# Convolving the first two 512-row blocks in eight 64x32 tiles of the matrix engine

## The chip, the cores and the metric

The kernel runs on one core of one Trainium2 chip. A core has a matrix engine (PE, with its weight loads shown as PEld), a vector engine (DVE), a scalar engine (ACT), GpSimd (POOL), and SyncE (SP), which only issues transfers. Results of PE land in PSUM, other data in SBUF. ACT, SP and POOL issue transfers too, each in the order of its own instruction stream, and a transfer that waits for something holds up what stands behind it on that engine.

The metric is the device time of one execution, in microseconds; the median of several runs is given. All times on a line of the profile are counted from the start of the profiled span.

## The reference

`x` is 8 x 4096 x 192 in float32. Each of 8 heads (24 channels each) has a filter of 7 taps, made by a softmax over its row of `weight`; a causal convolution along the sequence is followed by a gated feed-forward layer:

```python
w = np.exp(weight - np.max(weight, axis=-1, keepdims=True))
w = w / (np.sum(w, axis=-1, keepdims=True) + 1e-09)
x_pad = np.concatenate([np.zeros((B, pad, D)), x], axis=1)       # pad = 6
x_unf = x_pad[:, idx, :].reshape(B, S, K, H, group)              # 7 shifted rows
x = np.einsum('hk,bskhg->bshg', w, x_unf).reshape(B * S, D)      # 32768 x 192
gate = np.maximum(x @ w_gate, 0.0)                               # 192 -> 1536
val = x @ w_val
out = gate * val @ w_out                                         # 1536 -> 192
```

## The kernel before

The sequence is worked in 16 units of two windows of 512 rows, and every window holds two streams (batch b and batch b+4) on the two 64-row halves of the partitions. For each window the gate and value products are computed for 12 blocks f of the hidden dimension (`gate_val`, L602): per f, twelve matmuls for the gate and twelve for the value fill two PSUM tiles (in the first unit six and six, L621, each 64x128), ACT takes the ReLU of the gate (L632), DVE multiplies it with the value (L633). There are four PSUM tiles in turn, so block f+2 writes where block f was read. Then `project_turn` (L643) multiplies with `w_out`.

From the third window on the convolution is done by DVE, ACT and POOL on transposed x. The first two windows (blocks 0 and 1 below) cannot wait for that: they are convolved on PE (`conv_steps`, L370), with x as it lies in memory (rows on the partitions, channels along the free axis) as the stationary operand and a band matrix as the moving one. A band of head h has the seven taps along its diagonal. Window columns go in five steps of 106 (`STEP`), each from 112 rows of x (106 and 6 of the halo). A matmul takes one stream, one step and 32 channels, and writes 32 partitions of PSUM: a 128x32 tile, four of them side by side (`tile_position=(0, p0)`). Each group of 32 channels lies in two heads and is computed once with each head's band, the second over the first. That makes 5 steps x 3 chunks of 64 channels x 8 = 120 matmuls a block. One PSUM bank holds a chunk's 512 columns; an eviction (`evict`, L395) copies it to float16: for block 0 ACT, DVE, ACT, for block 1 ACT three times.

The order around it is written out by hand (manual schedule). At the start SP and ACT issue the five float32 pieces of x of block 0 (`load_raw`, L106; tiles prod1 to prod5), and ACT casts them to float16 (`cast`, L118). SP and ACT draw their transfers' semaphores from a ring of eight, DMAHW0 to DMAHW7; a ninth transfer waits until the first user of its semaphore has landed. Meanwhile the taps' exponential is taken on ACT (L278), DVE makes the products `prod`, `blk`, `blocks` (L287 to L299) from it, PE assembles the bands of eight heads by 24 matmuls (L335) in three PSUM parts, and DVE copies them out (L343). Block 0 is then convolved (L713), evicted, and feeds `gate_val`. Block 1 is convolved inside `gate_val` before block f = 10 (`CONV1`, L605). Its x is loaded by POOL in two transfers (one a stream, L97) that stand between the copies which double the weights onto the upper partitions (`pool_halves`, L233). `conv(2)` (L414) uses the same bands as stationary operand for the window after that.

Of the kernel before, what the change touches and what calls it, by code (L numbers as in the profile page):

```python
# [9 lines left out]
F16 = mybir.dt.float16  # L10
# [5 lines left out]
def kernel(  # L16
# [29 lines left out]
    GSUB = 5  # L46
    WARM = [(4, 4, 4, 1), (4, 3)]
    STEPS0 = [1, 0, 2, 3, 4]
    CONV1 = 10


# [29 lines left out]
    def staged(i, j):  # L81
        return stages[i][:, XH * j : XH * (j + 1)]

    def load_x(g, streams=range(2)):


        bp, toks = GROUPS[g]
        xt = staged(g // 3, g % 3).rearrange("p (j s d) -> p j s d", s=2, d=D)
        step = toks[1] - toks[0]
        rows = -(-(step + PAD) // 16) * 16  # L90
        for st in streams:
            src = bass.AP(
                tensor=x.tensor,
                offset=x.offset + ((bp + NB * st) * S + toks[0] - PAD) * D,
                ap=[[D, rows], [step * D, len(toks)], [1, D]],
            )
            nc.gpsimd.dma_start(out=xt[0:rows, 0 : len(toks), st, :], in_=src)  # L97
        return xt

    xts = {0: staged(0, 0).rearrange("p (j s d) -> p j s d", s=2, d=D)}  # L100
    ROWS = [SUB + PAD, 112, 112, 112, 96]
    raw = [
        apool.tile([128, 2 * LPOOL], FP, name=f"prod{jj + 1}")[:, 0 : 2 * D] for jj in range(GSUB)
    ]

    def load_raw(queue, jj):  # L106
        lo = STEP * jj - PAD
        p0 = max(0, -lo)
        queue.dma_start(
            out=raw[jj][p0 : ROWS[jj], :].rearrange("p (s d) -> p s d", s=2),  # L110
            in_=bass.AP(
                tensor=x.tensor,
                offset=x.offset + (lo + p0) * D,
                ap=[[D, ROWS[jj] - p0], [NB * S * D, 2], [1, D]],
            ),
        )

    def cast(copy, jj):  # L118
        copy(
            out=xts[0][0 : ROWS[jj], jj, :, :].rearrange("p s d -> p (s d)"),  # L120
            in_=raw[jj][0 : ROWS[jj], :],
        )

    HR = 128 // H
# [2 lines left out]
    nc.scalar.activation(out=early[:], in_=nc.const_aps.tensor(0.0, [128, 1], FP), func=ACTF.Exp)  # L127
    w8 = const.tile([H, KW], FP)
    nc.sync.dma_start(out=w8[:], in_=weight)
# [5 lines left out]
    nc.vector.memset(zeros[:], 0.0)  # L135
# [25 lines left out]
    with nc.allow_low_precision("one of the terms is not zero"):  # L161
        nc.vector.tensor_reduce(
            out=Z[:, 112 : 112 + HR],
            in_=eye[:].rearrange("p (g i) -> p i g", i=HR),
            axis=mybir.AxisListType.X,
            op=ALU.add,
        )
# [39 lines left out]
    raised = [raised[0][:, 0, :], raised[1][:, 0, :], held[:, 1, :]]  # L207
    for part, heads in zip(raised, BANDS):
        nc.tensor.matmul(
            out=part[:, 0 : SUB * len(heads)],  # L210
            lhsT=zeros[:],
            rhs=none(len(heads), SUB),
            start=True,
            stop=False,
            skip_group_check=True,
        )
# [106 lines left out]
    lane_load(0, range(1, 2))  # L323
    for jj in STEPS0[3:]:
        cast(nc.scalar.copy, jj)

    bands = [const.tile([128, len(heads), SUB], F16, name=f"band{heads[0]}") for heads in BANDS]
    for part, heads, to, copy in zip(
        raised, BANDS, bands, [nc.vector.tensor_copy] * 3
    ):  # L330
        n = len(heads)
        for j in range(128 // HR):
            s0 = HR * j - PAD
            lo, hi = max(0, -s0), min(BW, SUB - s0)
            nc.tensor.matmul(  # L335
                out=part[:, 0 : SUB * n].rearrange("p (h t) -> p h t", t=SUB)[:, :, s0 + lo : s0 + hi],
                lhsT=Z[:, 112 - HR * j : 240 - HR * j],
                rhs=blocks[:, heads[0] : heads[0] + n, lo:hi],
                start=False,
                stop=(j == 128 // HR - 1),  # L340
                skip_group_check=True,
            )
        copy(out=to[:].rearrange("p h t -> p (h t)"), in_=part[:, 0 : SUB * n])  # L343

    tap = const.tile([128, NCH, KW], FP)

# [18 lines left out]
            both_halves(nc.sync.dma_start, 10, Wv)  # L365

    def band(h):
        return bands[h // 3][0 : SUB + PAD, h % 3, :]

    dense, xcs = {}, {}  # L370

# [5 lines left out]
    def conv_steps(g, ps, c, steps):  # L377


        for jj in steps:  # L380
            col = STEP * jj
            n = min(STEP, WIN - col)
            rows = n + PAD
            for second in range(2):
                for st in range(2):
                    for k2 in range(2):
                        k = 2 * c + k2
                        h0, h1 = 32 * k // G, (32 * k + 31) // G
                        h, m = (h0, G * h1 - 32 * k) if second else (h1, 32)
                        p0 = 64 * st + 32 * k2  # L390
                        nc.tensor.matmul(  # L391
                            out=ps[p0 : p0 + m, 0, col : col + n],
                            lhsT=xts[g][0:rows, jj, st, 32 * k : 32 * k + m],
                            rhs=band(h)[0:rows, 0:n],
                            start=True,  # L395
                            stop=True,
                            tile_position=(0, p0),
                            skip_group_check=True,
                        )

    def evict(copy, g, ps, c):
        copy(out=dense[0][:, g, c, :], in_=ps[:, 0, :])  # L402

    def conv(g):

# [304 lines left out]
    for c, steps in (  # L710
        (0, STEPS0[:3]), (1, STEPS0[:3]), (0, STEPS0[3:4]), (1, STEPS0[3:4]), (0, STEPS0[4:]), (1, STEPS0[4:]), (2, STEPS0)
    ):
        conv_steps(0, first[c], c, steps)  # L713
    both_halves(nc.vector.tensor_copy, 0, Wg)
    both_halves(nc.vector.tensor_copy, 0, Wv)
    for c, copy in enumerate((nc.scalar.copy, nc.vector.tensor_copy, nc.scalar.copy)):
        evict(copy, 0, first[c], c)
# [85 lines left out]
```

## Time and profile before

| what | value |
|---|---|
| median of three runs | 762.4 us (761.5 to 762.61) |
| the profiled execution's own time | 762.03 us |
| its span | 760.3 us |
| PE busy | 756.3 us (99%) |
| DVE busy | 675.5 us (89%) |
| ACT busy | 610.0 us (80%) |
| POOL busy | 461.5 us (61%) |
| first matmul of the feed-forward part | at 7.98 us |
| block 1 convolved | from 21.11 us, 1.60 us |

The span is what lies between the first and the last instruction of the trace; the execution's own time is 1.7 us more. In the chain of waits each piece was released by the piece before it. In a timeline, a row has the start, the duration, the engine, line and operation, the number of instructions merged into it, and in brackets how long the engine stood idle before and what released it. The rows named SPq, ACTq and POOLq are issues of transfers, not their landings.

### The profile page before, as it was taken

How to read it: one execution, taken by the hardware profiler on the slowest of the kernel's cores; microseconds unless marked ns; L12 is line 12 of the kernel's file. 1: busy time of each engine (PE TensorE's matmuls, PEld its weight loads, DVE VectorE, ACT ScalarE, POOL GpSimd, SP SyncE). 2: the span in 40 equal slices, each digit the busy share in tenths (PEclk: the TensorE clock that was granted, in tenths of full speed). 3: DMA queues.
4: the chain of work that ended last, by engine and by line, in shares of the span. 5: the costliest groups of instructions: out<-in, count | busy, mean ns of one | idle time of the engine just before them, and what ended most of it. 6: DMA issues, size and time to landing. Idle time of an engine off the chain costs nothing.

```text
span 760.3 us, 30529 instructions
## 1 busy us (share of the span) xinstructions
PE 756.3 (99%) x13723; PEld 457.7 (60%) x13723; DVE 675.5 (89%) x647; ACT 610.0 (80%) x680; POOL 461.5 (61%) x311
## 2 busy tenths in 40 slices
PE   9999999999999999999999999999999999999998
PEld 5555555566666666666666666666666666666658
DVE  7889989998998989989999899998999989897891
ACT  7897887878878788887877878788797887877671
POOL 8729649195591946829377392874919659193600
PEclk9999999999999999999999999999999999999999
DMA  9953532345324443334434324352233532240302
GB/s 142 139 66 91 80 85 46 43 96 75 85 44 52 98 66 85 54 62 83 60 85 71 66 67 55 85 85 73 52 49 93 77 86 44 23 100 9 85 2 85
DMA packets 153714, 54.07 MB, mean 71 GB/s; under 512 B 148912, under 2 KB 153584, under 8 KB 153584
## 3 DMA queue, kind: packets, MB, share of 16 engines
q1 hardware_dynamic: 117152, 37.61, 21.8%
q0 software_dynamic: 35808, 14.07, 16.3%
q8 instruction: 107, 1.75, 1.0%
q10 hardware_dynamic: 624, 0.44, 0.2%
q14 instruction: 23, 0.19, 0.1%
HBM read 28.98 MB, written 25.17 MB: 71 GB/s over the span
## 4 chain that ended last, share of the span: by engine, by line
PE 99%; DVE 0%; ACT 0%; issue 0%
PE ps L621 65%; PE ps L643 31%; PE ps L686 2%; PE ps L391 0%; PE ps L193 0%; PE ps L335 0%; PE ps L414 0%; ACT xc L402 0%; PE ps L203 0%; DVE prod L287 0%; ACT out_s L697 0%; DVE blk L294 0%; DVE blocks L299 0%; ACT e L278 0%; DVE mx L275 0%
## 5 line engine op out<-in xcount | busy, mean ns | idle before, releaser
L633 DVE TENSOR_TENSOR hT<-gr,ps 128x1024 f16<-128x1024 f16 (+1 forms) x385 | 468.9, 1218 | 35.8 <-ACT gr L632 8.7
L632 ACT ACTIVATE gr<-ps 128x1024 f16<-128x1024 f32 (+1 forms) x385 | 392.8, 1021 | 114.7 <-PE ps L621 114.6
L550 POOL TENSOR_TENSOR prod<-prod,prod 128x896 f32<-128x896 f32 x145 | 302.8, 2088 | 251.3 <-DVE prod L584 242.2
L621 PE MATMUL ps<-xc,Wg 64*64 64x512 f16 (+1 forms) x4464 | 318.6, 376 | 0.2 <-ACT xc L402 0.2
L621 PE MATMUL ps<-xc,Wv 64*64 64x512 f16 (+1 forms) x4464 | 318.6, 376 | 0.0
L643 PE MATMUL ps<-hT,Wo 64*64 64x512 f16 x4320 | 235.8, 376 | 0.0
L621 PEld LDWEIGHTS <-Wv 64*64 64x64 f16 (+1 forms) x4464 | 150.0, 106 | 98.7 <-DVE hT L633 0.3
L621 PEld LDWEIGHTS <-Wg 64*64 64x64 f16 (+1 forms) x4464 | 146.6, 107 | 102.0
L643 PEld LDWEIGHTS <-Wo 64*64 64x64 f16 x4320 | 138.5, 107 | 94.4
L538 ACT ACTIVATE prod<-x_r,tap 128x1024 f32<-128x1024 f16 (+2 forms) x195 | 182.7, 1017 | 0.0
L574 DVE SCALAR_TENSOR_TENSOR acc<-x_r,tap,acc 128x1024 f32<-128x1024 f16 (+3 forms) x150 | 118.0, 853 | 0.0
L661 DVE STREAM_TRANSPOSE out_s<-ps 128x1024 f32<-128x1024 f32 x45 | 56.1, 1248 | 28.4 <-PE ps L643 24.4
L550 POOL TENSOR_TENSOR xc<-prod,prod 128x896 f16<-128x896 f32 x29 | 60.7, 2092 | 2.3
L479 POOL COPY x_p<-x_e 128x1536 f16<-128x1536 f16 (+1 forms) x32 | 42.2, 1349 | 0.0
L251 POOL DMA_DIRECT2D x_e<-in_x_dram x30 | 26.6, 890 | 0.0
L574 DVE SCALAR_TENSOR_TENSOR xc<-x_r,tap,acc 128x1024 f16<-128x1024 f16 (+3 forms) x30 | 25.2, 839 | 0.0
L563 ACT ACTIVATE acc<-x_r,tap 128x1024 f32<-128x1024 f16 (+3 forms) x30 | 22.5, 801 | 0.0
L656 ACT COPY turned_by<-ps 128x2 f32<-128x2 f32 x45 | 7.0, 154 | 16.8 <-PE ps L643 14.8
L686 PEld LDWEIGHTS <-hT 128*128 128x128 f16 x192 | 15.8, 98 | 0.4 <-issue 0.4
L686 PE MATMUL ps<-Wo,hT 128*128 128x192 f16 x192 | 16.0, 246 | 0.0
L697 ACT COPY out_s<-ps 128x768 f32<-128x768 f32 (+2 forms) x5 | 3.2, 638 | 12.7 <-PE ps L686 12.7
L697 DVE COPY out_s<-ps 128x192 f32<-128x192 f32 x1 | 0.4, 357 | 13.3 <-PE ps L686 13.3
(61 smaller groups left out, 74.6 us busy)
## 6 DMA issues: line engine op xcount, KB each, us to landing
out_dram<-out_s SPq DMA_DIRECT2D x125, 192.0 KB
x_e<-in_x_dram POOLq DMA_DIRECT2D x28, 384.0 KB, 5.8
x_r<-x_p SPq DMA_TRANSPOSE x116
prod<-in_moe_w_out_dram POOLq DMA_DIRECT2D x1, 576.0 KB, 9.1
out_dram<-out_s SPq DMA_DIRECT2D x5, 96.0 KB
out_s<-in_x_dram POOLq DMA_DIRECT2D x2, 210.0 KB, 6.2
out_s<-in_x_dram POOLq DMA_DIRECT2D x2, 192.0 KB, 6.6
x_e<-in_x_dram POOLq DMA_DIRECT2D x2, 192.0 KB, 3.8
```

The lines of the kernel that those rows point to most:

```text
L251: nc.gpsimd.dma_start(out=xe[:, 0:n, st, :, :].rearrange("p j c r -> p j (c r)"), in_=bass.AP(tensor=x.tensor, offset=x.offset + row * D, ...
L479: nc.gpsimd.tensor_copy(out=xp[:, js, :, st, :], in_=xe[:, js, st, :, :])
L538: nc.scalar.activation(out=both(prods[b, k], b, at, n), in_=shifted(b, c, k, t, n), func=ACTF.Copy, scale=tap[:, c, k : k + 1],)
L550: nc.gpsimd.tensor_tensor(out=acc if k < KW - 1 else xcs[b][:, w, :, :].rearrange("p c t -> p (c t)")[:, LDVE : NCH * WIN], in0=acc, in1=p ...
L563: nc.scalar.activation(out=both(accs[b], b, at, n), in_=shifted(b, c, 0, t, n), func=ACTF.Copy, scale=tap[:, c, 0:1],)
L574: nc.vector.scalar_tensor_tensor(out=result(b, at, n) if k == KW - 1 else both(acc, b, at, n), in0=shifted(b, c, k, t, n), scalar=tap[:, c ...
L621: nc.tensor.matmul(out=pss[i][q : q + M, st, :], lhsT=W[64 * st : 64 * st + 64, c, 128 * f + q : 128 * f + q + M], rhs=xcb[64 * st : 64 * ...
L632: nc.scalar.activation(out=gr[:, sts], in_=pss[0][:, sts], func=ACTF.Relu)
L633: nc.vector.tensor_tensor(out=h[:, f, sts], in0=gr[:, sts], in1=pss[1][:, sts], op=ALU.mult)
L643: nc.tensor.matmul(out=ps[64 * st : 64 * st + 64, b, :], lhsT=Wo[64 * r : 64 * r + 64, f, p, :], rhs=hs[b][64 * r : 64 * r + 64, f, st, :] ...
L661: nc.vector.transpose(out=o[:].rearrange("p t (b d) -> p b t d", b=2)[:, :, :, 32 * p : 32 * p + 32], in_=ps[:].rearrange("p b (t c) -> p ...
L686: nc.tensor.matmul(out=ps[:, i // 2, D * (i % 2) : D * (i % 2) + D], lhsT=h[:, f, st, 128 * q : 128 * (q + 1)], rhs=Wo[:, f, :, :].rearran ...
```

## The change

Blocks 0 and 1 are convolved with 64-row pieces. A window of 512 columns is cut into two halves of 256 (`HALF`); each half is cut into five pieces of 58 columns (`PIECE`, the last one 24), and each piece needs 64 rows of x (58 and 6). Pieces of the first half lie on partitions 0 to 63 and those of the second on 64 to 127, so a matmul takes one of eight 64x32 tiles, `tile_position=(64 * r, p0)`. The halves go to different PSUM banks. There are 240 matmuls a block in place of 120, of 58 (or 24) columns in place of 106 (or 88).

The band is built at 58 columns a head (`near`), for both partition halves at once (a copy of the identity block in `Z`, columns 176 on, does this): 12 matmuls in place of 24. The wide band that `conv(2)` needs (`large`) is cleared by DVE at the start and filled by two transfers on SP from `near`.

x of block 0 comes in ten transfers in place of five. The first has 58 rows (64 less the halo of 6, which is set to zero). The last two steps are cast for stream 0 by ACT and for stream 1 by DVE. x of block 1 comes in four POOL transfers in place of two. Block 1's second chunk is evicted by DVE in place of ACT.

```diff
-    ROWS = [SUB + PAD, 112, 112, 112, 96]
+    LAST = 64 + HALF - PIECE * (GSUB - 1) + PAD
+    ROWS = [64 + PIECE + PAD] * (GSUB - 1) + [LAST]
...
-    def load_raw(queue, jj):
-        lo = STEP * jj - PAD
+    def load_raw(queue, jj, r):
+        lo = HALF * r + PIECE * jj - PAD
         p0 = max(0, -lo)
+        n = min(64, -(-(ROWS[jj] - 64) // 32) * 32) if r == 0 else ROWS[jj] - 64
         queue.dma_start(
-            out=raw[jj][p0 : ROWS[jj], :].rearrange("p (s d) -> p s d", s=2),
+            out=raw[jj][64 * r + p0 : 64 * r + n, :].rearrange("p (s d) -> p s d", s=2),
...
-    for queue, steps in ((nc.scalar, (1, 2)), (nc.sync, (0, 3, 4))):
-        for jj in steps:
-            load_raw(queue, jj)
+    for queue, pieces in (
+        (nc.scalar, ((1, 0), (1, 1), (2, 0), (2, 1))),
+        (nc.sync, ((0, 0), (0, 1), (3, 0), (3, 1), (4, 0), (4, 1))),
+    ):
+        for jj, r in pieces:
+            load_raw(queue, jj, r)
...
+    large = const.tile([128, H, SUB], F16, name="large")
+    nc.vector.memset(large[:], 0.0)
+    nc.vector.memset(raw[GSUB - 1][32:64, :], 0.0)
...
+    nc.vector.tensor_copy(out=Z[:, 176 : 176 + HR], in_=Z[:, 112 : 112 + HR])
...
-    xts[1] = load_x(1, range(1))
+    xts[1] = load_x(1, halves=((0, 0), (1, 0)))
     for s in (3, 4, 5):
         pool_halves(s)
-    load_x(1, range(1, 2))
+    load_x(1, halves=((0, 1),))
     for s in (6, 7):
         pool_halves(s)
+    load_x(1, halves=((1, 1),))
     lane_load(0, range(1))
...
     for jj in STEPS0[3:]:
-        cast(nc.scalar.copy, jj)
+        cast(nc.scalar.copy, jj, slice(0, 1))
...
-        copy(out=to[:].rearrange("p h t -> p (h t)"), in_=part[:, 0 : SUB * n])
+        nc.vector.tensor_copy(
+            out=near[:, heads[0] : heads[0] + n, :].rearrange("p h t -> p (h t)"), in_=part[:, 0 : PIECE * n]
+        )
+    for jj in STEPS0[3:]:
+        cast(nc.vector.tensor_copy, jj, slice(1, 2))
+
+    for t in range(0, SUB, PIECE):
+        n = min(PIECE, SUB - t)
+        nc.sync.dma_start(out=large[t : t + n + PAD, :, t : t + n], in_=near[0 : n + PAD, :, 0:n])
...
-                        nc.tensor.matmul(
-                            out=ps[p0 : p0 + m, 0, col : col + n],
-                            lhsT=xts[g][0:rows, jj, st, 32 * k : 32 * k + m],
-                            rhs=band(h)[0:rows, 0:n],
...
-                            tile_position=(0, p0),
...
+                        for r in range(2):
+                            nc.tensor.matmul(
+                                out=ps[p0 : p0 + m, r, col : col + n],
+                                lhsT=xts[g][64 * r : 64 * r + rows, jj, st, 32 * k : 32 * k + m],
+                                rhs=near[64 * r : 64 * r + rows, h, 0:n],
...
+                                tile_position=(64 * r, p0),
...
-                    conv_steps(1, ps, c, range(GSUB))
-                    evict(nc.scalar.copy, 1, ps, c)
+                    conv_halves(1, ps, c, range(GSUB))
+                    evict_halves((nc.scalar.copy, nc.vector.tensor_copy)[c % 2], 1, ps, c)
```

How the change moves instructions is seen at three places. A row has the line, the operation, output and input tiles, the output's shape, and the semaphores that the instruction waits for (DVE_49 and its like are the engines' own counters). The first place is the start of SP's stream. In the names `prod_86` to `prod_90` are the five pieces' tiles, steps 0 to 4. Before:

```order
L129 DMA w_93<-in_weight_dram 8x7
L109 DMA prod_86<-in_x_dram 112x2x192
L109 DMA prod_89<-in_x_dram 112x2x192
L109 DMA prod_90<-in_x_dram 96x2x192
L354 DMA tap<-wn 24x1x7 [waits Pool_49]
```

After the change:

```order
L144 DMA w_93<-in_weight_dram 8x7
L124 DMA prod_86<-in_x_dram 58x2x192
L124 DMA prod_86<-in_x_dram 64x2x192
L124 DMA prod_89<-in_x_dram 64x2x192 x2
L124 DMA prod_90<-in_x_dram 32x2x192 [waits DMAHW0_49]
L124 DMA prod_90<-in_x_dram 30x2x192 [waits DMAHW2_49]
L372 DMA large<-near 64x8x58 [waits DMAHW3_49,DVE_49]
L372 DMA large<-near 60x8x54 [waits DMAHW4_49]
L383 DMA tap<-wn 24x1x7 [waits DMAHW5_49,Pool_49]
```

The weight takes DMAHW0, the 58-row piece DMAHW1 and the 64-row piece behind it DMAHW2, so the last two pieces of x wait for landings, and two transfers stand ahead of the taps. The second place is the start of ACT's stream. Before:

```order
L109 DMA prod_87<-in_x_dram 112x2x192
L109 DMA prod_88<-in_x_dram 112x2x192
L278 ACTIVATE e<-ps,mx 128x7 [waits DVE_49]
L281 ACTIVATE total,sm<-e 128x8 [waits Activation_49]
L119 CAST out_s<-prod_87 112x384 [waits DMAHW3_49]
```

After the change:

```order
L124 DMA prod_87<-in_x_dram 64x2x192 x2
L124 DMA prod_88<-in_x_dram 64x2x192
L124 DMA prod_88<-in_x_dram 64x2x192 [waits DMAHW1_49]
L300 ACTIVATE e<-ps,mx 128x7 [waits DVE_49]
L303 ACTIVATE total,sm<-e 128x8 [waits Activation_49]
L134 CAST out_s<-prod_87 128x384 [waits DMAHW5_49,DMAHW3_49]
```

The fourth transfer that ACT issues waits for DMAHW1, the semaphore of SP's 58-row piece; the exponential stands behind it. The third place is DVE's stream from block 0's eviction to beyond block 1. Before:

```order
L402 CAST xc<-ps 128x512 [waits PE_49]
L231 COPY Wg<-Wg 64x3x128 [waits DMASW2_49]
L231 COPY Wv<-Wv 64x3x128 [waits DMASW3_49]
L633 TENSOR_TENSOR hT<-gr,ps 128x512 [waits PE_49,Activation_49]
L633 TENSOR_TENSOR hT<-gr,ps 128x512 [waits Activation_49]
L633 TENSOR_TENSOR hT<-gr,ps 128x1024 [waits PE_49,Activation_49] x9
L611 MEMSET ps 128x1 [waits DVE_49]
```

After the change:

```order
L430 CAST xc<-ps 128x512 [waits PE_49]
L253 COPY Wg<-Wg 64x3x128 [waits DMASW2_49]
L253 COPY Wv<-Wv 64x3x128 [waits DMASW3_49]
L663 TENSOR_TENSOR hT<-gr,ps 128x512 [waits PE_49,Activation_49]
L663 TENSOR_TENSOR hT<-gr,ps 128x512 [waits Activation_49]
L663 TENSOR_TENSOR hT<-gr,ps 128x1024 [waits PE_49,Activation_49] x9
L430 CAST xc<-ps 128x512 [waits PE_49]
L641 MEMSET ps 128x1 [waits DVE_49]
```

An eviction of block 1 now stands on DVE between the product of block f = 9 and the one-element write that passes a PSUM tile on.

More of the change, by code (lines that the diff above doesn't have):

```diff
@@ L48 @@
     STEPS0 = [1, 0, 2, 3, 4]
+    HALF = WIN // 2
+    PIECE = 58
     CONV1 = 10
@@ L209 @@
         nc.tensor.matmul(
-            out=part[:, 0 : SUB * len(heads)],
+            out=part[:, 0 : PIECE * len(heads)],
             lhsT=zeros[:],
-            rhs=none(len(heads), SUB),
+            rhs=none(len(heads), PIECE),
             start=True,
@@ L324 @@
     for jj in STEPS0[3:]:
-        cast(nc.scalar.copy, jj)
[L327 to L330, printed above, removed]
+        cast(nc.scalar.copy, jj, slice(0, 1))
+    near = const.tile([128, H, PIECE], F16, name="near")
+    for part, heads in zip(raised, BANDS):
         n = len(heads)
-        for j in range(128 // HR):
+        for j in range(64 // HR):
             s0 = HR * j - PAD
-            lo, hi = max(0, -s0), min(BW, SUB - s0)
+            lo, hi = max(0, -s0), min(BW, PIECE - s0)
             nc.tensor.matmul(
-                out=part[:, 0 : SUB * n].rearrange("p (h t) -> p h t", t=SUB)[:, :, s0 + lo : s0 + hi],
+                out=part[:, 0 : PIECE * n].rearrange("p (h t) -> p h t", t=PIECE)[:, :, s0 + lo : s0 + hi],
                 lhsT=Z[:, 112 - HR * j : 240 - HR * j],
@@ L367, in band @@
     def band(h):
-        return bands[h // 3][0 : SUB + PAD, h % 3, :]
+        return large[0 : SUB + PAD, h, :]
     dense, xcs = {}, {}
@@ L375, with conv_halves @@
     PLACE |= {6: (1, 0, 0), 7: (1, 0, 1), 2: (1, 1, 0), 5: (1, 1, 1)}
[L377 to L382, printed above, removed]
+    def conv_halves(g, ps, c, pieces):
+        for jj in pieces:
+            col = PIECE * jj
+            n = min(PIECE, HALF - col)
             rows = n + PAD
@@ L712 @@
     ):
-        conv_steps(0, first[c], c, steps)
+        conv_halves(0, first[c], c, steps)
     both_halves(nc.vector.tensor_copy, 0, Wg)
@@ L716 @@
     for c, copy in enumerate((nc.scalar.copy, nc.vector.tensor_copy, nc.scalar.copy)):
-        evict(copy, 0, first[c], c)
+        evict_halves(copy, 0, first[c], c)
     both_halves(nc.vector.tensor_copy, 1, Wg)
```

37 lines of the change are left out of this document (25 added, 12 removed).

## The prediction

> **What bounds the kernel now.** First the page's totals and its chain of waits:
>
> ```profile
> span 760.3 us, 30529 instructions
> PE 99%; DVE 0%; ACT 0%; issue 0%
> ```
>
> PE sets the end nearly alone, so only what stands ahead of its unbroken run can change, or what PE itself does. The chain in order of time, over the first 24 us, shows both:
>
> ```profile
> 3.15 0.28 ACT e L278
> 3.45 0.33 DVE prod L287
> ...
> 4.57 1.22 PE ps L335 x24
> 5.78 1.54 PE ps L391 x70
> ...
> 7.35 0.59 ACT xc L402
> ...
> 7.98 13.20 PE ps L621 x120
> 21.18 1.53 PE ps L391 x120
> ```
>
> The exponential (3.15), the products, the bands, block 0 and its first eviction follow on each other; at 7.98 the feed-forward part starts, and block 1 takes 1.53 us out of it. So the sum has four terms: when the exponential starts, how long it is from there to the first L621, at what rate PE then runs, and what block 1 costs. It is made against the profiled execution's own 762.03 us, 0.37 below the median.
>
> **The exponential.** It is on ACT, behind ACT's transfers. After the change the fourth of these waits until SP's 58-row piece has landed, and behind it stand the exponential, the row sum and all casts; DVE's products, the bands and block 0 wait for these. The timeline:
>
> ```profile
> 0.81 0.41 SPq L129 DMA_DIRECT2D w<-in_weight_dram  x1
> 0.88 0.90 ACTq L109 DMA_DIRECT2D prod<-in_x_dram  x2
> 1.28 1.34 SPq L109 DMA_DIRECT2D prod<-in_x_dram  x3
> 2.32 0.50 PEld L203 LDWEIGHTS ps<-w,rows 8*128 8x128 f32 x2 [0.52 <-POOL prod L159]
> 3.66 0.50 ACT L119 CAST out_s<-prod 112x384 f16<-112x384 f32 x1
> 4.75 1.75 ACT L119 CAST out_s<-prod 118x384 f16<-118x384 f32 x4 [0.60 <-DMA prod<-in_x_dram]
> ...
> q10 hardware_dynamic: 624, 0.44, 0.2%
> ```
>
> A tiny transfer (the weight) is issued at 0.81 and used at 2.32: at most 1.51 us from issue to landing. ACT's queue q10 carried 624 packets in 0.2% of 16 engines' 760.3 us, 39 ns each. The 58-row piece is issued at 1.28 and has 58 x 2 = 116 packets. Spread evenly over 16 engines it lands at 1.28 + 1.51 + 0.3 = 3.1; cut into equal shares it has only two, 58 packets each, and lands at 1.28 + 1.51 + 2.3 = 5.1; if the 16 packets that ACT's pieces put on the same engines go in between, at 5.7. The kernel's pieces so far (112 and 96 rows) all have 16 equal shares, so no row decides. I take 5.1: the weight's 8 rows and the pieces fit equal shares, and 58 is the first count here that has hardly any. Then ACT issues its transfer (0.45, half of the row's 0.90), and the exponential starts at 5.55 in place of 3.15: **+2.4** (+0.4 to +3.0).
>
> [...]
>
> Ahead of that, DVE has two more clearings, the wide band (448 words a partition) and 384 more, and a 16-column copy:
>
> ```profile
> 0.89 0.11 DVE L135 MEMSET zeros<- 128x64 uint32 x1 [0.89 <-PEq L787]
> 1.97 0.37 DVE L162 TENSOR_REDUCE Z<-eye 128x16 f16<-128x128 f32 x1 [0.96 <-POOL Z L158]
> 5.15 1.22 DVE L343 CAST band<-ps 128x336 f16<-128x336 f32 x3 [0.25 <-PE ps L335]
> ```
>
> 64 words take 0.11, so 832 take at most 1.4 us, of which 0.96 is idle now. The rest delays POOL's weight loads by half a microsecond at most; the later exponential hides it. Without that cover it is part of the first rival.
>
> **From the exponential to the first L621.** PE's own rows at the start:
>
> ```profile
> 2.33 0.59 PE L203 MATMUL ps<-w,rows 8*128 8x7 f32 x2
> 2.85 0.93 PE L193 MATMUL ps<-const-bfloat16-1.0 128*128 128x512 bf16 x2
> 3.57 0.95 PE L209 MATMUL ps<-zeros 128*128 128x336 f16 x3
> 5.71 2.12 PE L391 MATMUL ps<-band,out_s 112*32 112x106 f16 x120
> ```
>
> It is 2.56 us to the first conv matmul (5.71) now. Half of the first band's eight matmuls go (4 x 1.22/24 = 0.2), and its copy has 174 columns in place of 336 (162 x 1.22/896 = 0.2): 2.2, so block 0 starts at 7.75. From there it is 2.27 us to 7.98 now: 1.62 to the end of the first chunk's matmuls, 0.59 eviction, the rest handing over. The rate of one matmul, by windows:
>
> ```profile
> 5.70:6.95 1.25, 1.25 (x63) 1.24 (x64) 1.14 (x4) 0.80 (x2) 1.25 (x3) 1.00 1.13 116
> 6.95:7.75 0.80, 0.80 (x76) 0.73 (x64) 0.31 (x1) 0.40 (x1) 0.80 (x2) 1.00 0.97 87
> 21.10:22.64 1.54, 1.54 (x122) 1.45 (x120) 1.47 (x2) 1.32 (x3) 1.54 (x3) 1.00 1.18 106
> ```
>
> The same matmuls pass at 19.8 ns each up to 6.95 and at 10.5 after it: PE runs at half speed first, though the page's clock column says 1.00. An eight-tile matmul has 58/106 of the columns and twice the tiles: 0.27 of that, 5.4 ns slow and 2.9 ns fast, if nothing but the array counts. The other bound is the fastest that weight load and matmul pairs are seen to pass, 10.5 ns. I take 8 ns, between, since the pairs in the rows were held up by columns and not by issue. The first chunk ends with the 144th of 240 matmuls: 1.15 us (0.8 to 1.5). The casts end later: DVE's three band copies (0.25 each, from 7.45) and two half casts (0.25 each) reach to 8.7, then 16 matmuls, the pipeline's 0.2 and the eviction's 0.59 follow: L621 starts at 9.65 in place of 7.98, **+1.67** (-0.1 with a landing at 3.1, +2.3 with 5.7).
>
> **PE's speed.** Full speed came at 6.95, 4.1 us after 2.85; ahead of that PE had only the two seven-column matmuls L203 for half a microsecond. After the change PE has nothing from 4.1 (L209 has 464 columns in place of 896) to the bands at 5.55 + 1.4 = 6.95. If the count starts there, full speed comes at 11.05, and the 1.4 us of feed-forward before that lose half: **+0.7**. The bounds are 0 (it comes at 6.95 regardless) and +1.7 (6.1 us as from the first matmul at 0.85). [...]
>
> **Block 1.** 240 pairs at 2.9 to 10.5 ns are 0.7 to 2.5 us against 1.53; at 8 ns 1.9. But PE cannot use a short one:
>
> ```profile
> 7.44 0.69 DVE L402 CAST xc<-ps 128x512 f16<-128x512 f32 x1 [0.57 <-PE ps L391]
> 20.33 2.52 DVE L633 TENSOR_TENSOR hT<-gr,ps 128x1024 f16<-128x1024 f16 x2
> 21.80 1.67 ACT L402 CAST xc<-ps 128x512 f16<-128x512 f32 x3 [0.21 <-PE ps L391]
> 23.30 0.81 PE L621 MATMUL ps<-xc,Wv 64*128 64x512 f16 x6
> ```
>
> The second chunk's PSUM tile is the one that block f = 10 fills with values, at 23.30 now, and ACT had emptied it before. After the change DVE does that behind the product of f = 9, which ends at 22.85: 22.85 + 0.69 = 23.54, so the values come **+0.25** late even where the matmuls are free. With 1.9 us of matmuls it is +0.4, and 10.5 ns a pair makes +1.0. I take **+0.4**.
>
> **Hidden.** POOL issues two more transfers:
>
> ```profile
> 9.35 0.86 POOL L97 DMA_DIRECT2D out_s<-in_x_dram  x1
> 10.73 0.50 POOL L231 COPY Wg<-Wg 64x384 f16<-64x384 f16 x1 [0.53 <-DMA Wg<-in_moe_w_gate_dram]
> 16.74 0.91 POOL L251 DMA_DIRECT2D x_e<-in_x_dram  x1
> Wg<-in_moe_w_gate_dram POOLq DMA_DIRECT2D x1, 144.0 KB, 4.8
> 40.93 0.79 PEld L414 LDWEIGHTS <-band 118*112 118x112 f16 x8 [0.42 <-issue]
> ```
>
> Each costs about 0.8. The first meets POOL's idle 0.53; with the second the last piece of block 1 is issued at about 17.3 and lands by 22.1 (144 KB took 4.8, it has 120). With the shifted start block 1 is due at 23.5; unshifted, at 21.2, it would wait 0.9. SP's two band transfers stand ahead of the taps, but the wide band is first read at 40.93.
>
> Sum: 1.67 + 0.7 + 0.4 = +2.8, so 764.8 on the profiled execution, and 765.1 as a median.
>
> **The rivals.** *One: the 58 rows spread evenly* and land at 3.1. For it: nothing forbids 4 rows an engine. Against: 58 is not a multiple of 16. The exponential comes at 3.55, the start moves by -0.1, full speed by at most 0.5, block 1 costs 0.4 and its late piece up to 0.9: +1.0, 763.4. *Two: PE stays slow longer.* With the upper bound of 1.7 in place of 0.7 it is 766.1. For it: the new gap of 2.8 us is longer than the one at 2.4. *Three: pairs pass no faster than now.* Block 0 gains nothing (+0.4 more) and block 1 costs +1.0: 766.1. For it: no row shows pairs below 10.5 ns. *Four, faster:* the array alone counts in both blocks. Block 0's first chunk takes 0.8 in place of 1.62 and block 1 0.7 in place of 1.53: -1.65, 760.7. It decides only if the 58-row piece lands by 2.7, so that the exponential keeps its 3.15, and if DVE empties block 1's chunk by 22.5; the end of f = 9 at 22.85 speaks against it. That the change does not do what it says I exclude: the instruction order shows 240 matmuls a block.
>
> **How the numbers follow.** About 0.2%, 1.5 us, is what a measurement of this kernel can tell from no change. The forecast has 0.5 (764.0 to 766.0), rival one 0.2, two 0.15, three 0.1, four 0.05. Slower by over 0.2% (above 763.9) are the forecast, two and three, 0.75, less the low edge of the forecast: 0.7. Rival one is within: 0.25 with that edge. Four is faster: 0.05. The range from 762.7 (rival one without a late piece) to 767.0 (both slow cases in part) leaves out four and the tails.
>
> **What would show it.** Right: ACT's exponential at 5 to 6 us with a wait for a transfer ahead, the first L651 at 9 to 10 us, the L651 matmuls slow for a while, the values of f = 10 waiting for DVE's L430, and an unchanged rest. Wrong: an exponential before 4 us, first L651 matmuls at full speed, or block 1 with its follow-up in less than 1.5 us; then the median is near or below 763.

## The result and the profile after

The changed kernel takes 780.3 us (median of four runs, 779.8 to 782.7) against 762.5 (761.5 to 762.7): 1.0242 times as long, 95% interval 1.022 to 1.0265. The prediction said 765.1 and slower, so the sign held and the size did not: +17.8 where its sum had +2.8. The profiled execution has 780.13 us around a span of 778.3, that is +18.0 in the span. Its page:

```profile
span 778.3 us, 31008 instructions
PE 97%; DMA 1%; issue 1%; ACT 0%; SPq 0%
q8 instruction: 109, 1.79, 1.0%
```

Two things are new in the shares of the chain: a transfer (DMA), and 1% of "issue" (0% before), time in which PE waited for nothing that the profile shows. The chain of waits over the first 45 us shows both:

```profile
1.28 5.45 DMA prod<-in_x_dram
...
6.75 3.54 DMA prod<-in_x_dram
...
10.30 0.52 ACT out_s L134
...
10.87 1.86 PE ps L419 x142
12.73 2.66 issue
...
33.02 4.76 issue
```

Before, nothing of this kind stood in the chain: block 0, the eviction, L621 at 7.98, and block 1 in 1.53 us. Now the chain begins with two transfers of x, one behind the other, and PE stops once within block 0 and twice within block 1. ACT's and PE's timelines give the exact starts:

```profile
2.31 5.04 ACTq L124 DMA_DIRECT2D prod<-in_x_dram  x2
7.40 0.27 ACT L300 ACTIVATE e<-ps,mx 128x7 f32<-128x7 f32 x1 [5.10 <-DMA prod<-in_x_dram]
10.30 1.02 ACT L134 CAST out_s<-prod 128x384 f16<-128x384 f32 x3 [1.49 <-DMA prod<-in_x_dram]
```

```profile
9.59 0.40 PE L419 MATMUL ps<-near,out_s 64*32 64x58 f16 x32
10.87 1.86 PE L419 MATMUL ps<-near,out_s 64*32 64x58 f16 x167 [0.89 <-ACT out_s L134]
15.39 0.53 PE L419 MATMUL ps<-near,out_s 64*32 64x58 f16 x41 [2.66 <-issue]
15.85 0.61 PE L651 MATMUL ps<-xc,Wg 64*128 64x512 f16 x2
...
30.22 1.00 PE L419 MATMUL ps<-near,out_s 64*32 64x58 f16 x95
31.58 1.43 PE L419 MATMUL ps<-near,out_s 64*24 64x58 f16 x128 [0.36 <-issue]
37.78 0.38 PE L419 MATMUL ps<-near,out_s 64*8 64x58 f16 x17 [4.76 <-issue]
38.09 1.46 PE L651 MATMUL ps<-xc,Wg 64*128 64x512 f16 x6
```

Block 1's 240 matmuls come as 95, 128 and 17. PE's clock changed too. The next rows are PE's in three stretches, the feed-forward matmuls (L651) alone: length, busy time and count of PE and of its weight loads, granted clock, DMA share, GB/s.

```profile
15.85:18.55 2.70, 2.70 (x14) 1.04 (x16) 1.00 1.46 178
18.55:30.20 11.65, 11.65 (x110) 5.34 (x104) 1.00 1.17 137
38.10:42.40 4.30, 4.30 (x22) 1.54 (x24) 0.50 0.36 73
```

A matmul takes 193 ns in the first stretch, 106 in the second and 195 in the third. The clock column shows the half clock in the third only. The first lies ahead of the trace's first clock record (full clock from 18.56), and where there is no record the column shows 1.00, as it did for the slow start before the change.

Four stretches therefore hold the whole difference. The following table is from the starts of PE's matmuls in the traces (before, after and the runs below). "f 0 to 9" is from the first to the 120th feed-forward matmul; "block 1" from the 120th to the 121st; "next 280" the 280 matmuls of PE behind that. All later stretches agree within 0.02 us in every kernel. (In e3 and e7 two thirds of block 1 lie within f 0 to 9.)

| kernel | first L621/L651 | f 0 to 9 | block 1 | next 280 | median, us |
|---|---|---|---|---|---|
| before | 7.98 | 12.82 | 1.84 | 24.84 | 762.5 |
| after | 15.85 | 14.07 | 8.17 | 26.98 | 780.3 |
| e1 106 rows | 11.85 | 13.91 | 1.83 | 24.82 | 767.0 |
| e2 split columns | 11.14 | 14.43 | 7.62 | 26.21 | 774.0 |
| e3 block 1 spread | 16.13 | 16.50 | 3.63 | 26.24 | 778.5 |
| e4 48 and 10 rows | 16.26 | 13.93 | 6.63 | 27.65 | 778.6 |
| e5 ACT freed | 16.26 | 15.06 | 6.20 | 26.52 | 779.8 |
| e6 70 pairs ahead | 13.64 | 15.50 | 7.43 | 26.28 | 778.8 |
| e7 all four | 12.02 | 20.91 | 1.07 | 25.20 | 773.3 |
| e8 one pass | 12.67 | 15.22 | 1.67 | 25.20 | 769.0 |
| e9 output weights late | 16.91 | 14.48 | 6.61 | 26.25 | 779.4 |
| e10 best of change | 11.97 | 17.84 | 4.95 | 26.35 | 774.9 |
| e11 before, weights late | 8.39 | 13.05 | 1.83 | 24.82 | 762.3 |
| e12 one pass, 48 and 10 | 10.75 | 15.31 | 1.69 | 25.19 | 767.2 |

After less before: +7.87, +1.25, +6.33 and +2.14, together 17.6. The other 0.5 (the spans differ by 18.07) stands behind PE's last matmul and was not looked into.

### The profile page after: what moved, and what is told of

Read it like the earlier page. It is cut to its first block, busy times and chain, and to the rows that moved or that the text cites. A ratio compares the mean times of both kernels' runs of the same rounds, so it can differ in the third digit from the quotient of the medians.

```text
span 778.3 us, 31008 instructions
## 1 busy us (share of the span) xinstructions
PE 760.6 (98%) x13951; PEld 457.6 (59%) x13951; DVE 679.8 (87%) x653; ACT 609.3 (78%) x679; POOL 462.8 (59%) x313
## 3 DMA queue, kind: packets, MB, share of 16 engines
q8 instruction: 109, 1.79, 1.0%
## 4 chain that ended last, share of the span: by engine, by line
PE 97%; DMA 1%; issue 1%; ACT 0%; SPq 0%
PE ps L651 64%; PE ps L673 30%; PE ps L716 2%; DMA prod<-in_x_dram 1%; PE ps L419 1%; PE ps L444 0%; ACT out_s L134 0%; SPq L144 0%; ACT out_s L727 0%
## 5 line engine op out<-in xcount | busy, mean ns | idle before, releaser
L651 PE MATMUL ps<-xc,Wg 64*64 64x512 f16 (+1 forms) x4464 | 320.5, 377 | 0.0
L651 PE MATMUL ps<-xc,Wv 64*64 64x512 f16 (+1 forms) x4464 | 320.1, 377 | 0.0
L651 PEld LDWEIGHTS <-Wv 64*64 64x64 f16 (+1 forms) x4464 | 150.3, 106 | 100.0 <-issue 2.4
L651 PEld LDWEIGHTS <-Wg 64*64 64x64 f16 (+1 forms) x4464 | 146.2, 107 | 103.8 <-issue 2.4
L419 PE MATMUL ps<-near,out_s 64*32 64x58 f16 (+7 forms) x480 | 5.6, 201 | 8.8 <-issue 7.8
```

Of the source, the lines that this page charges most:

```text
L651: nc.tensor.matmul(out=pss[i][q : q + M, st, :], lhsT=W[64 * st : 64 * st + 64, c, 128 * f + q : 128 * f + q + M], rhs=xcb[64 * st : 64 * ...
```

## The theory after the result, and its rivals

**Transfer.** The 58-row piece comes in two shares, the last of which lands at 6.73; ACT's fourth transfer, the exponential and the casts wait for it. The trace's semaphore events show the two: apart from one at 1.71, right behind the issue, the piece's semaphore rises at 6.54 and at 6.73 only. Before the change the 112-row piece in its place made its semaphore rise sixteen times, from 3.59 to 4.67. In the changed kernel's trace the weight's 8 rows have, behind such an early rise, eight (2.06 to 2.16), the 30-row piece of x fifteen (9.16 to 10.46) and the 60-row band transfer fifteen (16.41 to 18.53); the pieces of 32 and 64 rows have sixteen.

**Instruction supply.** PE's instructions come by queue q8: 1.79 MB in 109 packets is 16.4 KB each. By the pages PE and PEld together have 27902 instructions after the change and 27446 before, 109.0 and 107.2 times 256, and before the change q8 had 107 packets:

```profile
q8 instruction: 107, 1.75, 1.0%
```

In all runs that stop for "issue", PE stops ahead of its 223rd, 351st, 479th or 607th matmul (one later in e2), in steps of 128: 128 pairs of a weight load and a matmul are 256 instructions. So a packet is a block of 256 instructions, and where 128 pairs take 1.4 us PE is at the end of a block before the next is there. The kernel before had nearly as many packets, but the 120 pairs of its block 0 or 1 never crossed more than one border between instruction blocks in a row.

**Rivals.** The eight-tile shape itself makes PE stop; or the stops belong to the place in the program, where something unseen is awaited.

## The experiments

**e1: 106 rows first, in the kernel before.**

```
-    ROWS = [SUB + PAD, 112, 112, 112, 96]
+    ROWS = [112, 112, 112, 112, 96]
```

The first piece begins at partition 6, behind the halo, so 112 in place of 118 (`SUB + PAD`) leaves it 106 rows.

> The kernel before, with one number changed: the first piece of x on SP has 106 rows (2 x 53) in place of 112 (16 x 7). Two-shares theory: its 212 packets go through two of the 16 engines, 106 each at 33 to 50 ns, so it lands 3 to 5 us later than now (at 7 to 10 us in place of 4.7), the exponential stays at 3.15, block 0 stands until that piece is cast, and the first L621 starts 2 to 4 us later: 765 to 767 us. Even-spread rival: 16 engines take 6 or 7 rows each, nothing moves by more than 0.3 us: 762 to 763.

Measured: 767.0 us, ratio 1.0061 (1.0046 to 1.0076), at the upper edge of what two shares gave. The chain and ACT's timeline of this run:

```profile
2.31 7.68 DMA prod<-in_x_dram
...
11.92 14.21 PE ps L621 x120
```

```profile
8.20 1.45 ACT L119 CAST out_s<-prod 112x384 f16<-112x384 f32 x3 [3.53 <-DMA prod<-in_x_dram]
```

One piece of 106 rows is enough, in the old shape. Its semaphore rises at 8.08 and 8.12, again twice (from the issue at 1.28, less the weight's 1.51, 50 ns for each of 106 packets, the upper end of the 33 to 50 expected), and the last piece of x, which SP issues behind them at 2.31, is held back until 9.99. The first term's cause is shown for 58 and 106 rows: two shares, where 112 rows have sixteen.

**e2: twice as many matmuls in the old shape.** Each convolution matmul of the kernel before is cut into two column halves; nothing else changes.

```
-                        nc.tensor.matmul(out=ps[p0 : p0 + m, 0, col : col + n], ..., rhs=band(h)[0:rows, 0:n], ...)
+                        for c0, c1 in ((0, n // 2), (n // 2, n)):
+                            nc.tensor.matmul(out=ps[p0 : p0 + m, 0, col + c0 : col + c1], ..., rhs=band(h)[0:rows, c0:c1], ...)
```

> The kernel before, with each of the 240 conv matmuls cut into two of 53 (44) columns on the same 128x32 tile: the array has the same columns to do, PE twice the instructions. Instruction-supply theory: PE's instructions come in 16 KB blocks of 256, a block takes 3.5 us or more to come, and 480 instructions pass in less than 3; so block 0 shows an idle stretch of PE of 2 to 3 us and block 1 one of 3 to 5 us put down to 'issue', each pair outside of them takes about 11 ns, and PE falls back to half clock after block 1: 770 to 776 us. Rival, the eight-tile shape itself (64-row tiles, two PSUM banks) stops PE: no idle stretch, each block 0.3 to 1.2 us longer: 763 to 765.

Measured: 774.0 us, 1.0157 (1.0142 to 1.0172). Its chain:

```profile
5.70 2.01 PE ps L392 x152
7.71 2.90 issue
10.61 0.60 PE ps L392 x43
...
25.95 2.65 PE ps L392 x178
28.60 4.15 issue
32.75 0.51 PE ps L392 x21
```

The same stops, 2.90 and 4.15 us, with four tiles of 112x32 and with x loaded as before. The clock falls to half behind both, as expected (12.15 to 15.56 and 32.63 to 36.04 by the clock records). The pairs are slower than the 11 ns expected, 13.2 ns (152 in 2.01) and 14.9 (178 in 2.65). The eight-tile shape falls as the cause of the stops; the number of instructions in a row remains.

**e4 and e5: the transfer in two ways.** e4 loads the 58 rows as 48 and 10; e5 leaves them and moves ACT's fourth transfer to SP.

```
e4  +        for q0, q1 in ((p0, n),) if p0 == 0 else ((p0, n - 10), (n - 10, n)):
    +            queue.dma_start(out=raw[jj][64 * r + q0 : 64 * r + q1, :]..., in_=...)
e5  -        (nc.scalar, ((1, 0), (1, 1), (2, 0), (2, 1))),
    +        (nc.scalar, ((1, 0), (1, 1), (2, 0))),
    -        (nc.sync, ((0, 0), (0, 1), (3, 0), (3, 1), (4, 0), (4, 1))),
    +        (nc.sync, ((0, 0), (0, 1), (3, 0), (2, 1), (3, 1), (4, 0), (4, 1))),
```

> The changed kernel, with SP's 58-row piece loaded as 48 and 10 rows; ACT's fourth transfer still waits, now for the 48 rows. Two-shares theory: they land by about 3.5 to 4, the exponential starts at 4 to 4.6 in place of 7.40, the last piece's cast no later than 8, the first L651 at 11.5 to 12.5 in place of 15.85 (the idle stretch of PE in block 0 stays): 775 to 777 us. Rival, ten transfers in place of five are what is late, however they are shared out: exponential at 6.5 or later, within 1 us of the changed kernel's 780.3.

> The changed kernel, with ACT's fourth transfer moved to SP, so that the exponential stands behind no wait; the 58-row piece stays. If the wait on ACT is what is late: exponential at 3.2, first L651 about 4 us earlier (at 11.5 to 12): 776 us. If the slow piece itself also holds block 0 up: exponential at 3.2, bands by 6, then PE waits for the casts of the pieces that lie behind the slow one (7.5 to 9 us), first L651 at 12.5 to 14, 777 to 779 us.

Measured: e4 778.6 us, 1.0212 (1.0197 to 1.0227); e5 779.8, 1.0234 (1.0217 to 1.0251). Both are short of the gain expected, and the runs of e5 (778.9 to 780.7) overlap those of the changed kernel. e4's chain:

```profile
4.19 4.04 DMA prod<-in_x_dram
...
10.78 5.03 issue
15.80 0.52 PE ps L420 x31
```

In e4 the exponential starts at 4.84, the casts of the last pieces begin at 8.25 in place of 10.30, and the same matmul as before waits 5.03 us in place of 2.66: PE goes on at 15.80 in both e4 and e5, at 15.39 after the change. In e5 the exponential is back at 3.15, but one of the pieces of SP, which now issues seven, lands only at 12.21, and the stop behind it is still 2.29. An earlier front gains nothing while the instruction block sets the time.

**e3 and e6: the count of instructions moved.** e3 spreads block 1 over three places; e6 adds 70 tiny matmuls on PE while it waits, so that the border of a block falls ahead of block 0.

```
e3  -    CONV1 = 10
    +    CONV1 = [6, 8, 10]
    ...
    +            if u == 0 and w == 0 and f in CONV1:
    +                c = CONV1.index(f)
    ...
e6  +    FILL = 70
    ...
    +    for _ in range(FILL):
    +        nc.tensor.matmul(out=held[0:32, 0, 0:16], lhsT=many(32), rhs=many(16), start=True, stop=True)
```

> The changed kernel with block 1's three chunks ahead of f = 6, 8 and 10 instead of all three ahead of f = 10. Theory of instruction supply (PE takes instructions in blocks of 128 weight-load and matmul pairs, and a block comes some 4 us after PE reached the one before it): the two stops inside block 1 (0.36 and 4.76 us) shrink to 0 to 2 us together, since 24 feed-forward matmuls (2.6 us) now lie between two chunks, and with them the half-speed stretch behind block 1 goes: 772.5 to 775.5. Rival (eight tiles at once in themselves cost this, wherever they stand): 779 to 781.

> The changed kernel with 70 tiny matmuls (16 columns, 32 rows) put on PE while it waits for the exponential, so that PE reaches the start of the next instruction block before block 0 and not in it. Supply theory: the stop of 2.66 us in block 0 goes, the first L651 comes at 12.9 to 13.4 in place of 15.85; the block starts move by 70 matmuls in block 1 too, which then meets one stop of 2 to 3 us in place of 0.36 and 4.76: 772 to 776. Rival (the stop belongs to the work in block 0, not to a count of instructions): the stop stays, 779 to 782.

Measured: e3 778.5 us, 1.0208 (1.0183 to 1.0234); e6 778.8, 1.0231 (1.0189 to 1.0273). Both totals miss, to the slow side; e6, with one run of 783.5, is not clear of the changed kernel. The PE timeline of e3, then the one of e6:

```profile
32.93 0.66 PE L419 MATMUL ps<-near,out_s 64*32 64x58 f16 x63
35.95 0.38 PE L419 MATMUL ps<-near,out_s 64*8 64x58 f16 x17 [2.36 <-issue]
```

```profile
10.65 1.12 PE L422 MATMUL ps<-near,out_s 64*32 64x58 f16 x97 [0.84 <-ACT out_s L135]
12.48 1.22 PE L422 MATMUL ps<-near,out_s 30*32 30x24 f16 x111 [0.72 <-issue]
...
29.44 1.74 PE L422 MATMUL ps<-near,out_s 64*32 64x58 f16 x153
35.56 1.08 PE L422 MATMUL ps<-near,out_s 30*8 30x24 f16 x87 [4.38 <-issue]
```

The stops moved as a count of instructions says. In e3 the one of 0.36 is gone and the one of 4.76 is 2.36; in e6 the one of 2.66 is 0.72, the first L651 comes 2.2 us earlier, and block 1's borders are behind its 25th and 153rd matmul in place of the 95th and 223rd, each 70 earlier; it stops at the second alone. So the place in the program falls as the cause. What was wrong is the price: I had taken a block to come 4 us after PE entered the block ahead of it; in e6 it was 3.1 and 6.0 us (the table below). In e6 a stop of 1.41 also appeared in the feed-forward part, at the 351st matmul, and the stop in block 1 was 4.38.

**e8: the old number of matmuls in the new shape.**

```
-            for second in range(2):
+            for second in range(1):
```

> The changed kernel with the second of the two passes of each convolution chunk left out, so the channels of the lower head in each 32-channel strip get the upper head's band: a part of the convolution is not computed in these two blocks. 120 pairs a block in place of 240, in the same eight-tile shape. Supply theory: neither block 0 nor block 1 reaches a second block start in it, so no stop: first L651 at 12.0 to 12.7, block 1 with its 120 pairs at 11 ns 1.35 us: 766 to 769. Rival (the eight-tile shape itself causes the stops): half of the stops stay, 772 to 775.

The second pass is left out, so a part of the convolution of these two blocks is not computed. Measured: 769.0 us, 1.0084 (1.0061 to 1.0106), the upper edge of what the supply theory gave. Its chain has no stop in either block:

```profile
11.21 0.80 PE ps L419 x57
...
12.67 15.60 PE ps L651 x120
28.27 0.47 PE ps L419 x40
28.73 1.20 DVE hT L663
29.93 0.61 DVE xc L430
```

With e2 this closes the matter from both sides: many matmuls in the old shape stop, few in the new shape do not. Block 1 takes 1.67 us against 1.84. By the table the changed kernel has +3.18, -1.15, +6.50 and +1.78 over this run: the stops, the other 120 pairs of each block and the half clock behind block 1. The -1.15 is e8's own longer half clock, 5.04 us behind its first L651 against 2.71.

The last two lines of the chain are new. With the stops gone, the values of f = 10 wait for DVE, which evicts block 1's second chunk behind the product of f = 9:

```profile
30.59 0.82 PE L651 MATMUL ps<-xc,Wv 64*128 64x512 f16 x6 [0.20 <-DVE xc L430]
```

e12 below shows the same wait, 0.19.

**e9 and e11: does a block wait behind other transfers?** POOL's 576 KB of output weights are issued later, in the changed kernel (e9) and in the one before (e11).

```
-    nc.gpsimd.dma_start(out=plain..., in_=moe_w_out...)          # ahead of the unit loop
     ...
             lane_turn(0)
+            nc.gpsimd.dma_start(out=plain..., in_=moe_w_out...)  # and the two copies Wo behind front_conv()
```

> The changed kernel with POOL's 576 KB transfer of the output weights, in flight from 25.9 to 35.6 and so during block 1's stops, issued only behind POOL's copies x_p (about 32.5), and its two copies Wo behind the front lanes. Theory that an instruction block waits behind other transfers: asked for at 31.6 it now comes sooner, the long stop in block 1 falls from 4.76 to 1.5 to 3.5 us, and perhaps the half-speed stretch behind it is shorter: 775 to 778.5. Rival (the block takes its 4 to 7 us whatever else is moved): 779.5 to 781.

> The kernel before the change with the same transfer of the output weights moved, a control: before the change PE never stops for instructions in block 1, so by both theories the time stays, 761.5 to 763. If it moves by over 1 us, moving the transfer does something else too, and e9 is to be read against this run.

Measured: e9 779.4 us, 1.0238 (1.0222 to 1.0255); e11 762.3, 1.0002 (0.9993 to 1.0011). The control holds. e9's PE timeline:

```profile
33.41 1.34 PE L419 MATMUL ps<-near,out_s 64*24 64x58 f16 x128 [0.71 <-issue]
37.69 0.38 PE L419 MATMUL ps<-near,out_s 64*8 64x58 f16 x17 [2.93 <-issue]
```

The long stop fell to 2.93, within the range, but the time missed its own and lies 0.1 below the rival's; its runs (779.3 to 782.1) overlap those of the changed kernel. In the profiled execution the front was 1.06 later (the 58-row piece landed at 7.60 in place of 6.73) and f 0 to 9 took 0.41 longer, which gave back 1.5 of the 2.3 us won in and behind block 1. The next rows have the DMA busy share (the figure ahead of the last; it passes 1 where packets overlap) in the wait between PE entering an instruction block and the next packet's start: e9 in block 1, then e6 in block 0 and in block 1.

```profile
33.40:35.40 2.00, 1.34 (x128) 1.17 (x128) 0.79 (x3) 0.00 (x0) 1.73 (x3) 1.00 0.38 74
```

```profile
9.40:10.00 0.60, 0.39 (x32) 0.23 (x31) 0.60 (x3) 0.00 (x0) 0.60 (x2) 1.00 0.04 13
...
29.50:33.20 3.70, 1.68 (x154) 1.45 (x154) 1.60 (x2) 1.01 (x2) 2.17 (x4) 0.93 1.61 189
```

The following table is from the trace's records of single packets; PE enters an instruction block with its first matmul:

| run | PE enters a block | next packet starts | takes | PE goes on | in all |
|---|---|---|---|---|---|
| after, block 0 | 11.18 | 12.52 | 1.26 | 15.39 | 4.2 |
| after, block 1 | 31.58 | 33.73 | 2.56 | 37.78 | 6.2 |
| e4, block 0 | 9.13 | 13.56 | 0.88 | 15.80 | 6.7 |
| e6, block 0 | 9.42 | 10.00 | 0.88 | 12.48 | 3.1 |
| e6, block 1 | 29.54 | 33.23 | 0.94 | 35.56 | 6.0 |
| e9, block 1 | 33.42 | 35.35 | 0.95 | 37.69 | 4.3 |
| e10, block 1 | 30.20 | 31.29 | 1.14 | 33.83 | 3.6 |

From the packet's start to PE going on it is 2.2 to 2.9 us, or 4.0 where the packet itself took 2.56. The wait ahead of it was 0.6 to 1.9 us in these runs where the DMA engines were little used (share 0.04 to 0.39), and 1.3 to 4.4 where they were full (1.1 to 1.6). e2's two blocks, which the table leaves out, waited 1.41 and 3.58 at shares of 1.13 and 1.63. That leans to other transfers as the cause, but the two groups overlap, and the packet's engine is not in the records. From the changed kernel to e9 the share in block 1 fell from 1.62 to 0.38 and the wait only from 2.15 to 1.93; what became short is the packet itself, 0.95 in place of 2.56. Why a given block comes at 1.3 or at 4.4 stays open.

**e7, e10 and e12: causes taken away together.** e7 is e3, e4, e5 and e6 in one; e10 is e4, e5, e6 and e9; e12 is e4 and e8, so it too leaves out the second pass.

> The changed kernel with all causes found so far taken away at once: 58 rows as 48 and 10, ACT's fourth transfer on SP, 70 tiny matmuls ahead, block 1's chunks ahead of f = 6, 8 and 10. If the two-share transfer, ACT's wait and the instruction blocks are all there is, the exponential starts at 3.2 to 4.8, the first L651 comes at 10 to 11.5 (7.98 in the kernel before), and what is left over the kernel before is the late start and the pair rate of 11 ns (240 pairs 2.7 us, against 1.53): 766 to 769. If something else holds block 0 or 1, over 771.

> The changed kernel with 48 and 10 rows, ACT's fourth transfer on SP, 70 tiny matmuls ahead and the output weights late, block 1 in one piece ahead of f = 10. Against the run with all four, the waits that the spread block 1 brought (PE behind ACT's gr and DVE's hT, twice some 2.3 us) are gone and one stop of 2 to 4.5 us comes back. First L651 at 11 to 12.5; if the long stop is short (under 2.5 us): 767 to 770, if not: 770 to 774. Slower than the kernel before in any case, by the rate of the pairs and the late start.

> The changed kernel with both taken away together: the second pass left out (so a part of the convolution of the two blocks is not computed, 120 pairs a block), and the 58 rows loaded as 48 and 10. With the instruction blocks out of play the front should now follow the x pieces: exponential at 4.2 to 4.9, last cast at 8.2 to 8.8 in place of 10.6 to 11.2, first L651 at 9.7 to 10.6 (12.67 with one pass alone), 764 to 766.5, so that the two-share transfer is worth 3 to 4.5 us once the stop behind it is gone. If it stays at 767.5 to 769.5, the front is held by something else than the landing.

Measured: e7 773.3 us, 1.0137 (1.0114 to 1.016); e10 774.9, 1.0165 (1.0145 to 1.0186); e12 767.2, 1.0061 (1.0045 to 1.0078). Of e7's chain:

```profile
5.85 4.51 DMA prod<-in_x_dram
...
10.85 1.24 PE ps L423 x94
12.09 3.95 PE ps L655 x17
```

and of e12's:

```profile
4.23 4.48 DMA prod<-in_x_dram
...
9.29 0.80 PE ps L420 x59
...
10.75 15.68 PE ps L652 x120
```

All three miss to the slow side: e12 by 0.7 us, e7 by 4.3, and e10, whose stop in block 1 was short (2.05 us), by 4.9. Two things are common to them. The front hangs on the last piece of x: it lands at 10.36 in e7, though SP issued it at 5.85, and at 8.71 in e12. And PE runs at half speed long behind it: until 20.46 in e7, until 15.97 in e12, by the trace's clock records; f 0 to 9 takes 15.31 in e12 against 12.82, +2.5, with no stop in it. Why the full clock comes so late there stays open.

e7 and e10 were not free of stops either: PE stops for "issue" ahead of the 351st matmul, in the feed-forward part, for 0.81 us in e7 and 2.05 in e10, and e10 runs at half clock again from 17.40 to 20.81. The expectation of e10 also took too much for the spread block 1. The 2.3 us are the time of ACT's gr and DVE's hT in e7's chain (1.03 and 1.23); PE itself stands only some 0.2 us for them, three times.

e12 is what is left with neither the two-share transfer nor a stop: 5 us over the kernel before, 2.8 of it the later start and 2.5 the half clock. No variant comes near the kernel before.

## Why the prediction was right in sign and wrong in size

**The exponential: the cause right, the term too small.** The choice of two equal shares is shown (landing at 6.73; e1; e4, where 48 and 10 rows bring the exponential to 4.84). The price failed: 5.1 (at most 5.7) came from 39 ns a packet, an average over another queue. Issue to landing took 5.45 us, and 4.93 to 6.32 in e3, e5, e6, e8 and e9; less the 1.51 that the weight needed, that is 59 to 83 ns for each of 58 packets. The packets of 768 bytes on SP's queue q1 took 48 ns on average up to 12 us, which makes 2.8 of the 3.9 us. The other 1.1 is not shown; packets of other pieces between them would fit, and the forecast had those of ACT's pieces only in its bound. The exponential came at 7.40, +4.25 in place of +2.4.

**From the exponential to the first L651: one half right, one step missing.** Block 0 starts 2.19 us behind the exponential, where 2.2 was forecast. Then the prediction let the casts end on their own work, at 8.7; in fact ACT's own fourth transfer, issued only when the 58 rows had landed, lands at 10.28 and holds the casts and PE until 10.87. I had counted that transfer's issue time (0.45) and not its landing.

**The rate: rival three was right in the mean.** 167 pairs in 1.86 us at half speed (the feed-forward matmuls behind them still take 193 ns) and 128 in 1.43 at full are 11.1 and 11.2 ns, not 8. As it is the same at both speeds, the array alone is not what counts. Nor is 11 ns a floor: 64 neighbouring pairs start within 0.52 us in both blocks (from 10.87 and from 32.06), 8.1 ns each, and pauses of about 0.1 us between groups make the mean; what PE waits for in them was not looked into. 240 pairs take 2.7 us against 1.53; that was worth +1.2 in block 1 where I took +0.4.

**The missing term.** This is the step that failed most. No row of my sum asked whether the instructions are there; it let PE run through both blocks without a stop, which is a wait put at nothing without a reason. The stops cost 2.66 us in block 0 and 5.12 in block 1, 7.8 of the 18.0. "The same matmuls pass at so many ns each" was carried from 120 pairs in a row to 240, and the page's row of queue q8 stood there all along: 256 instructions in a packet, in a kernel whose 107 packets came some 7 us apart. 240 pairs at any of my rates run through nearly two instruction blocks in under 3 us. The sign does not hang on this term: without the stops, e8, with half the pairs, is still 0.84% (6.4 us) over the kernel before, by the front and the half clock.

**PE's speed.** The cost in f 0 to 9 is +1.25, inside the bounds of 0 to +1.7 and above the +0.7 taken; the doubling itself came at 18.56, far behind the 11.05 forecast and the 13.1 that belong to the bound of 1.7 (9.65 and twice 1.7). That the cost is still inside the bounds is luck in part: the first L651 was late as well, so that 2.71 us of feed-forward ran at half speed, where 1.4 was forecast. A second stretch was not foreseen at all: after the stop of 4.76 the clock fell to half (35.63 to 42.46), 22 matmuls in 4.30 us that take 2.3 at full speed, +2.0 of the +2.14 in "next 280". So "an unchanged rest" was wrong as well. By the clock records the full stretch ahead of the fall is 17.07 us and the half one 6.83; what sets these lengths was not shown.

**Block 1.** DVE's eviction of the second chunk, on which +0.25 rested, decided nothing in the changed kernel: it ran from 32.40 to 33.09, and PE stood for its instructions from 33.02 to 37.78. Where the stops are gone the forecast mechanism shows: PE waits 0.20 us for it in e8 and 0.19 in e12. POOL's two more transfers and SP's two band transfers cost nothing that shows, as forecast.

**The rivals.** One (even shares) and four (the array alone counts) fell; two names a cost that is real (+1.25 where it had +1.7) and a small part of the 17.8; three had the mean rate. None named the supply of instructions, and the range ended at 767.

## What to carry to other kernels

Before a change doubles the number of small matmuls in a row, set their time against that of a block of 256 PE instructions: here 128 pairs took 1.4 us and the next block 3 to 7, so that PE stopped, and every stop of 2.05 us or more at full clock was followed by a stretch at half clock. Look at what the row counts of transfers divide by: 112, 96 and 64 rows went in sixteen shares here, 58 and 106 in two, which held up the queue, the casts behind it and what those feed. Where a cost is averaged from other rows, its upper bound belongs in the range.

## What the hardware showed that I had not expected

- PE stops for "issue" only at borders that are 128 pairs apart (223rd, 351st, 479th, 607th matmul), where most of the pairs ahead passed in 11 to 15 ns; 3.1 to 6.7 us from entering an instruction block to having the next, in the seven cases of the table.
- Pairs in eight tiles of 64x32 with 58 columns pass in 11.1 to 11.2 ns in the mean, at half and at full clock alike, and 64 in a row in 8.1 ns.
- The transfer in two shares also slowed others. By the semaphore events, of the piece that SP issues next fourteen shares land by 4.94 and two at 7.52 and 7.56; before the change all sixteen landed from 4.61 to 5.38. That the two are on the same engines is inferred, since no record has the engine. The 58-row transfer itself took 4.93 to 6.32 us in six profiles.
